# A hand-ordered H3 and spectral mixing kernel: three groups of zero matmuls enter the table, and the whole order is written anew

## The chip, the cores and the metric

The kernel runs on one core of one Trainium2 chip. The metric is the device time of one execution in microseconds (us), the median of several runs. The profile is that of one more execution, with its own time.

The engines are named as in the profile: PE does matmuls (PEld are its weight loads), DVE is the vector engine, ACT the scalar engine, POOL the gpsimd engine, and SP issues most of the DMAs. The clock granted to PE is given as a share of full speed.

## What is computed

The reference mixes two branches by a gate, on a sequence of 2048 tokens with 640 channels, all in float32:

```python
g = sigmoid((x * gate_w).sum(-1))              # x is A_q
k_shift = causal depthwise conv of k, 4 taps
kv = k_shift * v
y = irfft(rfft(kv, 4096) * rfft(ssm_k, 4096))[:2048] + kv * ssm_D
a = q * y                                       # branch A
b = irfft2(rfft2(x) * (w_r + 1j * w_i))         # branch B, over tokens and channels
return g * a + (1 - g) * b
```

## The kernel before

All Fourier transforms are matmuls with constant matrices. A length of 2048 is split into 64 x 32, so each transform has two stages with a 32 x 32 block transpose by DVE between them (L319, L440, L652).

Branch A goes in five chunks c of 128 channels. `kv` (L576) makes the four-tap convolution times v for half a chunk: ACT scales k by each tap (L601) and POOL or DVE adds (L609), or, for chunk 0, ACT starts (L592) and DVE goes on in PSUM (L595); PE transposes the result (L624) and DVE multiplies it with v (L632). `s1` (L638, matmuls L649) is the first stage for kv ("Y") and for the filter ("H"), `amid` (L673, matmuls L685) the second stage and the product of both spectra: ACT copies one part out of PSUM (L694 or L696), and DVE (L700) or POOL (L702) multiplies. `asum` (L705, L709) adds parts, `is1a` (L712, matmuls L314, transpose L319) is the first inverse stage and `afin` (L726, matmuls L744) the second. Its unit "q" loads q and lets ACT scale it by the gate, eight small steps (L733); DVE multiplies with it (L751), and the result is added to the output in DRAM by an accumulating DMA from POOL (L762) or, for the last half of the last chunk, added by POOL to a kept piece (L758) and stored by SP (L760).

Branch B: `dfwd` (L361) is the transform over channels for two of 16 token groups: it loads xT, folds it by symmetric sums and differences (L340; a sum of 512 at L347, differences and sums of 256 at L348, L350 and L351, a small one of 128 through ACT L355 and DVE L356, or DVE alone at L358) and multiplies (16 passes of 128 rows at L371, 16 of 32 rows at L377); ACT copies the result into XX (L387 to L394). Then `b1` (L437, transpose L440), `bs2` (L456, with the weights w), `i1` (L314), and at the end `bfin`: units "u" (L498, L506, copied by ACT L517) and "dic" (L525, L530), whose results `bout` (L540) scales with the gate (ACT L547 to L550, DVE L553), adds (L555, L556, on POOL or DVE) and sends to the output (L568 from SP, L570 from POOL). `gate_cols` (L328 to L334) writes the gate's columns into the constant dfc, so the first fwd needs dfc and these small DVE steps.

The program has 993 steps. Each has a name (a unit such as fwd.4, kv.4.8, amid.3.1.0), one or two engines on which it can run, and buffers: eight PSUM banks ("ps"), eleven "a" buffers of 128 x 1088, five "s", one "k", one for the big constants s2b and is2b ("c1"). `order` (L210) reads the order from TABLE: an entry `i+a/b1/b2<j` issues step i on its alternative a, with its new buffers in slots b1 and b2, and makes it wait for step j. Every engine runs its own steps in that order, each waiting by semaphores for data and buffers; SP's DMA queue is in order too. Nothing is reordered at run time. Some loads that the order moves: xT of a group is 512 KB, dic 403.5 KB, a w 322 KB, a v 512 KB, is2b 2 MB.

At the start, while the first loads are on their way, PE runs 24 matmuls of a zeroed tile `wrm` (two passes each, L773).

Of the kernel before, what the change touches and what calls it, by code (L numbers as in the profile page):

```python
# [31 lines left out]
345/1 152/4/0 41 336/2 39 344 40+1<39 167/3 160/4 123/5 342 31+1/2/1 32 35 159 328/7 34 153 33 155 102+1/0/4 154 42+1/2/6 106/0 157 103+1 16/8 105+1  # L32
158 156 107 104+1 95+1/2/0 324/0 96+1 116/6 49 80+1/1/3 98+1 48 325 99/4 43 81<98 97 46 10/9 100 45 326 44 108/6/4 47 82 83 84/2 85 73+1/2/1 346 77/3
74+1 75<74 78 349/2 327/0 109 115 168/0/4 110 111 347/4 114 350 76 433/1 113 112 348 405/0 169 86+1/0/2 172/6 225/3 9/0 171 173 170+1 161+1/2/0 162+1
165/7 163+1 219/4 329/4/0 8 124+1/1/3 93 245/0 337/2 164<124 166 87 330 290/10 88 4 125 92 90 338 89 126 174/6/4 91 128/0 129 251/5 127 427/7
117+1/2/1 121/1 118+1 119+1 120+1 351/2/1 181 17/0/4 18 122 19+1<18 21 130/4/0 352 20+1 175 176 11/2/0 177 407/2 178 12 180 15 179 13 409/6 136 131
133 134 132 14 22+1/2/6 137 135 353/0 23 29 27 25 28 357/4 24 355/6 26 184/2 358 406/8 356 411/9 408<14 354 192/4 193 416/0 413/2 410 188/6 182 186/0
189 183 412 185 375/4 187 379/6 383/2 376/1 380/6 377 363/0 378 384/3 381+1 190/4 386 364/9 385 365+1 194/2 191 428+1 382+1 429/4/2 195 366+1 417/6
371/6 372/9 430 434+1 246/2 247/2/0 220/0 204/4 374+1 248 221/4/1 373+1 420/0 418/9 437/2 222 7 249 232/4 202/6 438 250 205 414/0/0 419 203 226/2
359/4 415 227/8 224 264/9 360/3 228/0/2 223 422/2 361 229 493/0 362 435/6 200/0 395/1 231 252/2 436 233/4 230 253/3 201 421 387/6 254/1/4 367/0  # L40
234/3/0 235 388/8 368/2 494/0 198/2 258/4 370 390+1 369 431/4 495/7 196/0 389 432 255<389 496 497/8 303/3 284/5 199 197 499/7 498+1 396 393/4 237<498
504/0 424/8 236 423 391/0 500 394 265/4 400/2 285/6 392 501/7 286/2/0 425/0 256 287 397/2 257 426 266/6 267/3/1 288 506/5 289 259/6 515/8 401 398 268
304/0 439/4/1 399 260/4/0 270 297/6 261 445/2 269 440 212/9 305/4 306/2/1 262 443/6 263 441/4 502/0/0 446 442 307 505/1 507 444 298/2 508/3 291/4
206/4 292/0 299/3/0 503 402/6 308 521/5 309 300 510/7 516+1 471/0 293/4/1 301 455/2 403 459/4 302 472/2 294 404 456/0 474 600/0 473 460/6 463/6 458
296 277/0 457 467/0 464/3 461+1 475/2 465 468/10 466 462 213/6 476/2 451/4 469 214/6 470 452/10 477 295<477 215/2/0 447/0 478 207/6 448/3 454+1<478
517/2/0 449 208/1/4 453+1 488/2 450 519/0 209 604/10 216 518 512/4 481/4 601/8 211+1 520 217<211 602/6 522+1 509+1 483/9 606/3 479/0 603+1 210+1 608/6
589/0 482 511<210 489 605 480 278/4 513/6 279/7 591/1 271/10 514 525/0 218 607 590/4 527/2/1 280/3/1 526 523/6 238/5 533/4 528 611/3 281 529/0 484
584/0 534 592 531/2 272/4 593/7 524 490/6 532 595/1 273/4/0 283 282 594 485/2 530 274 491 239/0 597/10 276 486 240/7 241/2/1 551/4 275 487 543/6 492
552/3 596 559/2 553 544/0 554 547/0 560/4 545 242 561 598/4/0 548/1 562 546 617/9 539/2 540/4 550+1 599 696/0 549 555/6 579/5 243+1 704/7 609/4 675/2
# [12 lines left out]
971 939 972 911/6/2 749 950/1 840 940/3 949 750 941 952 973 763+1 909+1/0/0 951 912 764+1 851 942 953 767/4 954 910 980/4<764 943 955/1 944 913+1/0/2
# [117 lines left out]
class _Plan:  # L180
# [41 lines left out]
def _body(ctx, tc, I, out):  # L222
# [21 lines left out]
    def ps(b):  # L244
        return banks[:, b.slot:b.slot + b.banks]
# [3 lines left out]
    mm = nc.tensor.matmul  # L249
# [39 lines left out]
    wrm = cst.tile([128, 128], F32, name="wrm")  # L289
# [286 lines left out]
    def kv(c, h, kvt):  # L576
# [23 lines left out]
        else:  # L600
# [172 lines left out]
            mm(ps(pw)[:, 0, :128], wrm, wrm, start=True, stop=True)  # L773
# [128 lines left out]
```

## Time and profile before

| | |
|---|---|
| median of 3 runs | 289.94 us (288.68 to 290.15) |
| the profiled execution's own time | 291.7 us |
| its span in the profile | 289.9 us |
| mean granted clock of PE | 0.98 |
| busy: PE, DVE, POOL, ACT | 258.9, 225.9, 205.8, 151.4 us |
| moved by DMA | 53.93 MB, mean 186 GB/s |

A row of the timeline reads: start, length, engine, line, operation, output and inputs, shapes, number of instructions, and in brackets how long the engine had been idle and what ended it. A row of the groups by line has the busy time, the mean of one instruction in ns, the idle time before them and its releasers. In the chain of waits, each piece is start, length, and what the end of the kernel hung on at that time.

### The profile page before, as it was taken

The numbers are of one execution on the slowest core, as the hardware profiler recorded it, in microseconds if no ns is written. First come the engines' busy times: TensorE is split into PE (matmuls) and PEld (weight loads), VectorE is DVE, ScalarE is ACT, GpSimd is POOL, SyncE is SP. The second block draws the span as 40 slices with busy tenths as digits, with TensorE's granted clock in tenths as the row PEclk, the third lists the DMA queues.
The fourth block names the chain that finished last, engine by engine and source line by source line (L and its number), as shares of the span: only waits on it lengthen the run. The fifth ranks groups of instructions, "written<-read, shape, count | busy, mean of one in ns | idle before, by whom it ended". The sixth has DMA issues, their size and how long they took to land.

```text
span 289.9 us, 9390 instructions
## 1 busy us (share of the span) xinstructions
PE 258.9 (89%) x4024; PEld 169.9 (59%) x4024; DVE 225.9 (78%) x284; ACT 151.4 (52%) x315; POOL 205.8 (71%) x206
## 2 busy tenths in 40 slices
PE   8784999989999899889999988999998998999750
PEld 8663797534554366534385323678766775888450
DVE  2689698497999799899999999993467857358670
ACT  2238349715456465756655763354594036486710
POOL 1362732367897998776996999858990876889872
PEclk9899799999999999999999999999999999999996
DMA  7999999370155785847558657292003397305788
GB/s 211 418 394 363 379 339 398 109 290 18 49 183 155 249 235 159 287 119 251 175 186 266 257 154 310 79 270 103 3 3 91 93 196 128 54 22 76 111 114 144
DMA packets 25432, 53.93 MB, mean 186 GB/s; under 512 B 1840, under 2 KB 13360, under 8 KB 24880
## 3 DMA queue, kind: packets, MB, share of 16 engines
q1 hardware_dynamic: 22048, 48.63, 48.9%
q0 software_dynamic: 3344, 4.72, 11.7%
q8 instruction: 31, 0.51, 0.7%
q14 instruction: 9, 0.07, 0.1%
HBM read 43.38 MB, written 9.96 MB: 184 GB/s over the span
## 4 chain that ended last, share of the span: by engine, by line
PE 64%; DVE 22%; issue 5%; ACT 3%; DMA 2%; POOL 1%; POOLq 1%; SPq 1%; ACTq 0%; DVEq 0%
PE banks L685 12%; PE banks L649 9%; PE banks L314 7%; PE banks L530 7%; PE banks L498 6%; PE banks L437 5%; PE banks L744 5%; PE banks L371 4%; DVE ZZ L652 3%; DVE XX L319 3%; DVE ZZ L319 3%; DMA a<-xT 2%; PE banks L525 2%; DVE s L468 2%; DVE ZZ L700 2%
## 5 line engine op out<-in xcount | busy, mean ns | idle before, releaser
L609 POOL TENSOR_TENSOR a<-a,a 128x1024 f32<-128x1024 f32 x21 | 50.1, 2392 | 13.7 <-ACT a L601 10.6
L652 DVE STREAM_TRANSPOSE ZZ<-banks 128x1024 f32<-128x1024 f32 x40 | 47.9, 1229 | 9.0 <-ACT XX L391 4.7
L601 ACT ACTIVATE a<-k,one 128x1024 f32<-128x1024 f32 x32 | 35.9, 1149 | 26.2 <-POOL a L609 9.7
L685 PE MATMUL banks<-ZZ,s2a 64*32 64x256 f32 x1280 | 41.0, 387 | 3.5 <-issue 1.3
L702 POOL TENSOR_TENSOR ZZ<-a 128x512 f32<-128x512 f32 x24 | 30.5, 1288 | 12.1 <-ACT a L694 10.9
L685 PEld LDWEIGHTS banks<-ZZ,s2a 64*32 64x32 f32 x1280 | 23.9, 104 | 17.5 <-issue 4.3
L553 DVE SCALAR_TENSOR_TENSOR s<-banks,om,s 128x322 f32<-128x322 f32 x32 | 17.4, 550 | 21.4 <-ACT s L550 20.9
L700 DVE TENSOR_TENSOR ZZ<-banks,s 128x512 f32<-128x512 f32 x40 | 25.3, 682 | 6.1 <-ACT s L696 5.9
L709 POOL TENSOR_TENSOR ZZ<-ZZ 128x512 f32<-128x512 f32 x21 | 26.4, 1283 | 3.0 <-DVE ZZ L700 2.9
L476 POOL TENSOR_TENSOR XX<-s,s 128x320 f32<-128x320 f32 (+1 forms) x29 | 24.3, 858 | 4.3 <-DVE ZZ L700 2.2
L371 PE MATMUL banks<-dfc,s 128*128 128x162 f32 x128 | 22.7, 335 | 4.9 <-POOL s L350 2.9
L314 PE MATMUL banks<-ZZ,one 32*64 32x512 f32 x448 | 26.6, 607 | 0.3 <-DVE XX L319 0.3
L319 DVE STREAM_TRANSPOSE ZZ<-banks 128x2048 f32<-128x2048 f32 x10 | 22.9, 2306 | 4.0 <-PE banks L314 4.0
L694 ACT ACTIVATE a<-banks 128x1024 f32<-128x1024 f32 x20 | 20.4, 1028 | 10.0 <-PE banks L685 9.0
L371 PEld LDWEIGHTS banks<-dfc,s 128*128 128x128 f32 x128 | 20.4, 211 | 7.6 <-POOL s L350 3.1
L733 ACT ACTIVATE a<-a,g 128x128 f32<-128x128 f32 x80 | 24.3, 391 | 0.9 <-DMA a<-q 0.9
L649 PE MATMUL banks<-a,one 64*128 64x512 f32 x80 | 21.1, 615 | 3.1 <-DVE ZZ L319 1.6
L744 PE MATMUL banks<-ZZ,is2a 128*64 128x128 f32 x320 | 19.5, 277 | 3.1 <-ACT a L733 2.8
L744 PEld LDWEIGHTS banks<-ZZ,is2a 128*64 128x64 f32 x320 | 18.1, 134 | 5.8 <-ACT a L733 3.7
L649 PE MATMUL banks<-kvt,one 64*128 64x512 f32 x80 | 20.0, 616 | 0.2 <-ACT a L694 0.2
L437 PE MATMUL banks<-XX,two 64*128 64x464 f32 (+1 forms) x88 | 19.8, 582 | 0.1
L530 PE MATMUL banks<-dic,s 128*128 128x161 f32 x128 | 19.6, 305 | 0.0
(83 smaller groups left out, 474.9 us busy)
## 6 DMA issues: line engine op xcount, KB each, us to landing
a<-xT SPq DMA_DIRECT2D x16, 512.0 KB, 9.6
k<-k SPq DMA_DIRECT2D x10, 704.0 KB, 5.3
a<-h SPq DMA_DIRECT2D x10, 544.0 KB, 5.1
a<-w SPq DMA_DIRECT2D x16, 322.0 KB, 3.8
a<-v SPq DMA_DIRECT2D x10, 512.0 KB, 5.8
a<-q SPq DMA_DIRECT2D x10, 512.0 KB, 4.9
out_dram<-a SPq DMA_DIRECT2D x8, 512.0 KB, 4.7
out_dram<-a POOLq DMA_DIRECT2D x16, 256.0 KB, 5.9
```

Source lines behind the costliest of these rows:

```text
L314: mm(p[h * 64:h * 64 + 64, j, :nd * 8], is1[r, c, :], v[r, h * 2 + ri, :, d0:d0 + nd, :].rearrange("p m d e -> p d m e"), start=(i == 0), ...
L319: nc.vector.transpose(by_col(x, d0, nd), p[:, :, :nd * 8].rearrange("p j (d i) -> p d j i", i=8))
L371: mm(v(q)[:, i, :CB], sb(f, 5, 128)[:, x], dfc[:, x], start=first and i == 0, stop=True, skip_group_check=True)
L437: mm(v()[:, b], m1b[r, ri], xv[r, ri, d0:d0 + nd], start=ri == 0, stop=ri == 1)
L530: mm(v(q)[:, i, :161], sb(u, 5, 128)[:, q], dic[:, q * 161:q * 161 + 161], start=first and i == 0, stop=True, skip_group_check=True)
L601: tap = lambda t, j: op([("ACT", act_us(1024), lambda: act(sb(t, 8, 128), K(j), AF.Copy, scale=sh[:, c, j:j + 1]))], r=[k, "one"], w=[t], ...
L609: either(1024, lambda o: o(sb(ts[x], 1024), sb(ts[x], 1024), sb(ts[y], 1024), op=OP.add), r=[ts[y]], w=[ts[x]])
L649: mm(ps(p)[:, b], m1[r], v[r], start=True, stop=True)
L652: op([("DVE", dve(1024), lambda: nc.vector.transpose(by_col(Z(z), u * 32, 32), ps(p).rearrange("p b (d n) -> p d b n", n=16)))], r=[p], w= ...
L685: apart(c, m, "mid", mm(ps(p)[j * 32:j * 32 + 32, h].rearrange("p (y r d) -> p y r d", y=2, r=2)[:, :, ri], s2a[r, k, ri * 32:ri * 32 + 32 ...
L700: alts = [("DVE", dve(512), lambda x=x, dst=dst, hv=hv: tt(dst(), V(part(ps(p), zy)), hv(), op=OP.mult))]
L744: mm(v[b * 64:b * 64 + 64, j, :], is2a[:, n2, :], row(Z(zh), n2), start=True, stop=True)
```

## The change

Three units "fill" are added behind the warm-up. Each runs five matmuls of the zeroed tile (ten passes) into a PSUM bank that nothing else reads. As they are declared right after steps 0 and 1, every later step has its number raised by three: step 64 becomes 67.

```diff
+FILL = 3
...
     pe(8.6, warm, "F", r=["wrm"], w=[pw], new=[pw])
+    for i in range(FILL):
+        unit("fill", i)
+        pf = new("ps")
+
+        def fill(pf=pf):
+            for _ in range(5):
+                mm(ps(pf)[:, 0, :128], wrm, wrm, start=True, stop=True)
+
+        pe(1.15, fill, "F", r=["wrm"], w=[pf], new=[pf])
```

The table is new from the first entry to the last. Its beginning and end:

```diff
-57/0 0 1/0 3 5 2 50/1 145/2 331/0 138/3 339/4 36/5 94/6 58+1/0/1 30/7 101/8 59+1 62/1 61+1 79/9 63 60<61 6 51+1/2/3 55/2 52+1 53+1 56 54+1 146+1/4/0
-64/4/6 150/3 147<146 151 148 149 139/2/4 332/0 333 334 71 143/2 65 66 67 140 340+1 70 144 69 335/10 341/6/0 68 142 141 37/1/3 38 323/0 343/2 72/0
...
+60/0 6 53/1 5 8 148/2 0 1/0 4/1 61+1/0/1 65/2 66 62<61 64+1 334/0 141/3 63<64 342/4 39/5 33/6 97/7 104/8 54+1/2/3 55+1 57+1 56<57 58/3 59 9 82/9
+149+1/4/0 150+1 152<150 151 153/4 154 142/2/4 143 67/6/2 335/0 336 337 146/5 147 73 343+1 344/4/0 144+1 145+1 74 346/2 40/1/3 68 69 70 72 41+1<40 43+1
...
+106+1 107+1 108+1 110 160 159 98+1/2/0 99+1 339/6 83+1/1/3 100+1 248/8 327/0 102/6 103 328 329 2/7 101<100 52 111+1/2/6 119/7 46 48 50 47 49 84 86 85
...
-880 945/6 981 768 946 956 957 948 914 769/4 915/1 947 916 917 958 918 925/0 924 919 926 983 927 770 985 920/9 982 922 921 928 923 929 930+1/8 881/0
-931+1 933 986/4 882 932<931 883 988 987 991+1 989+1 992 990
+923/7 924 772/4 773 931 932 926 933+1/8 934+1 936 3/2 935+1 925+1 950<925 884/2 885 886 960 989/4 990 992+1 993 991 994+1 995
```

Steps 2, 3 and 4 of the new numbering are the fills: 4 stands right behind the warm-up (bank 1), 2 between the matmuls of fwd.2 and fwd.8 (bank 7), 3 between is1.4.1 and afin.4.0 (bank 2). Read by unit, the rest changes as follows.

- PE keeps its sequence of stages; neighbours trade places (b1.1 before b1.0, amid.0.0.1 before amid.0.2.1, afin.3.8 before afin.3.0, and many more such pairs).
- The first five loads were fwd.5's xT, two, dfc, one, fwd.4's xT, and are now fwd.5's xT, two, fwd.4's xT, one, dfc. The loads of dic, of w for bs2.0.6 and of v for kv.0.8 now stand ahead of the xT of fwd.10, fwd.1 and fwd.0.
- 30 steps change between DVE and POOL. Thirteen of them are folds of the first fwd; the others are products and sums of amid, asum, bs2, kv.2.0 and dic. At the end, two small steps of dic.10 and dic.11 (L556) go from POOL to DVE, ahead of afin.4.0's product (L751), and one of dic.13 (L556, POOL) comes between afin.4.0's store and the last two additions (L758).
- The loads of q.4.0 and q.4.8 and their ACT scalings move forward. q.4.8 is scaled among the taps of kv.4.8, ahead of two of them, and q.4.0 after those of kv.4.0, ahead of amid.3.1.0; before, q.4.0 was scaled ahead of ACT's steps of dic.10 and q.4.8 as ACT's last step. On SP, is2b, q.4.0 and q.4.8 now stand ahead of q.2.8, q.2.0, h.3.1, h.3.0 and the k of kv.4.0.

No arithmetic on the data changes.

More of the change, by code (lines that the diff above doesn't have):

```diff
@@ L34 @@
[L34 to L49, printed above, removed]
@@ new lines @@
+173+1 164+1/2/0 168/7 165+1 169 166+1 167+1 96 95 13/1 7 228/0 254/3 127+1/1/3 128<127 129 130 90 92 93 94 91 332/0/0 333 340/6 341 430/2 416/5
+177/2/0 222/10 12/0 131/4 132 120+1/2/1 124/5 121+1 123+1 122+1 183 184 20/0/4 21 23+1<21 22+1 24 354/6/1 125 133/0/4 178 182 181 179 180 355 410/4
+409/6 14/2/0 15 18 17 16 25+1/2/6 134 135 137 138 136 411<16 140 356/4 357 139 32 360/0 26 31 27 358/6 359 29 10 28 361 30 189/4 195/2 191/6 185 190
+192 196 366/0 412/7 413 414/9 415 419/0 382/4 367/1 368 383/4 369+1<368 378/6 379/2 381 187/2 188 193/0 186 385+1 436/7 197/2 421/9 431+1 380 432/6/2
@@ new lines @@
+420/1 422 423/9 194 374/0 384+1 375/4 198 223/2 249/4 433 424 425/9 496/0 377+1 224/1/3 225 227 306/10 250/0/4 251 235/8 376+1 253 207/6 208 205/2 206
+226 252 434/4 435 417/6/0 418 229/0 427/2 370/2 255/4 230/4 231/2/1 232 234 233 371/3 373 372 256/6 257/0/4 258 386/6 387/3 388 389 203/0 204 267/5
+236/2 237/3/1 238 497/0 398/4 362/4 363/2 364 365 390/6 199/0 437+1 440/2 438/4 391/3 426 200 201/0 439 500/6 502/8 392+1 498/9 287/7 393+1 394/4
+261/3 499 501 240 503 441 260 507/0 508/9 239 518/6 519+1 202 396/0 399 395 268/4 288/6 397 259 403/8 289/2/1 290 291 292 504/7 428/0 429 269/1
@@ new lines @@
+270/3/0 271 509/2 510 273 300/1 272 400/2 401 402 293/5 262/6 263/4/1 264 266 265 404 442/0/1 443 446/4 444/2 445 448/6 449 511/3 307/0 308/2 309/2/0
+310 505/2/0 506 215/4 311 301/6 302/3/1 294/0 295/0 405/2 447 466/4 513/7 603/0 491/2 303 474/6 312 296/4/0 462/0 305 304 406 407 297 299 467/2 469
+468 475/1 477 476 463/10 209/1 458/2 459/3 460 461 464+1 465 470/4 471/0 473 472 478/6 479/5 481 298<481 216/2 217/10 218/2/1 480 454/0 455/8
+457+1<480 456+1 605/0 210/4 211/3/0 212 214 450/2 451/4 453 452 524/5 520/6/0 521 522/4 523 484/0 482/4 219 492 280/1 486/8 274/6 525+1 515/4 512+1
@@ new lines @@
+701/0 988 575 705/10 631 582/8 628/4 629 323/0 324 620/7 313/4 314 321/0 322 583 319/4 320 573 574 700/4 571 317/0 318 572 621+1 588 570 614/6 615+1
+315/4 316 688/0 702 690/0 704 689/2 706 691 692/10 694/0 883 580/0 581 578/4 579 616/0/1 622/2 623 624/4 618/6 625 617 589/2 584/4 619 642/0 643/1
+634/6 635/3 693 695 707/7 590 646/2 591 647/6 585 654/4 645 644 658/0 716/10 637 636 697/6/0 586 649 648 669<648 668 857/2/2 659/0 660 661 855+1/0/4
+655/0 657+1 656+1 858 698 678/3 856 708/6 709 638/2 639/6 640+1 641+1 666 667 650/0 651/1 653 652 670 671 859/6/4 861/3 860 803/0/0 801+1/2/1 872/2
@@ new lines @@
+862 710/2 863 804 722/0/0 864 865 871 874 873 662/6 875 876 877/8 879 878 880 723 802 805/2/4 663/5 665+1 664 673<664 806 683/4 818/4 776/0/2 817
+774+1/6/0 807/1 819 820 821 777 724/0 808 809 728/2 822 810 811 725 729 775 684 672 676/4 677 866/7 679 674/0 778+1/4/6 780/0 790 791/2 793 779 782
+781 812/0 814 813 815 867 711+1 675 685/0 686 687 680/2 712/0/2 868 783 717+1 792 726/4 794 681 720/2 682 795 796/6 798 784 889/6/1 727 887+1/4/3
+785/5 786 787 789 797 800 799 823/4 825 788 713 718/0 888 824 714/4 890 870 721 891/2/6 893/0 892 902 816 827 719 830/0/2 715 894 964+1/4/4 895 896
@@ new lines @@
+897 900/3 898/10 899 831 903/1 904 905 906 907 910 908/2 826 965 909 754/0 755/3 757 756 881 730/2 731/0 732 733 742/4 743/5 744 745 734/6 735/6
+737+1<745 901 738/0 739/3 741 740 736 763+1 911 758/2 759/0 760 761 769<761 828/4/1 829 962+1/0/0 963 764 832+1/6/4 844 845/3 765 966/2/0 834/1 762
+846 847 848 849 850/4 833 835 836 837 838 937/6/2 967 968/0 977 970 969 851+1 852<851 853 938 939+1/4/4 839/5 746/6 869 978/3 979 980 750/2 768 940
+841 840 842 971 972 973/6 975 981 982 747/1 748 749 974 751/8 752+1 753+1 766+1 767+1 976 843 983/0<767 941+1/4/0 952 942 953/0 943/1 955 954 944 945
```

22 lines of the change are left out of this document (7 added, 15 removed).

## The prediction

> **What bounds the kernel now.** I read the page first: the shares of the engines and the chain that ended last.
>
> ```profile
> span 289.9 us, 9390 instructions
> PE 258.9 (89%) x4024; PEld 169.9 (59%) x4024; DVE 225.9 (78%) x284; ACT 151.4 (52%) x315; POOL 205.8 (71%) x206
> PE 64%; DVE 22%; issue 5%; ACT 3%; DMA 2%; POOL 1%; POOLq 1%; SPq 1%; ACTq 0%; DVEq 0%
> ```
>
> PE is the first limit (64% of the chain), DVE the second (22%). PE stands still for 289.9 - 258.9 = 31 us, and the page's line of the granted clock dips twice in the first 36 us. Next I read the timeline of PE there, then the table of short windows around each drop (columns: length, busy time of PE, its weight loads, DVE, ACT, POOL, then granted clock, DMA share, GB/s).
>
> ```profile
> 1.06 7.68 PE L773 MATMUL banks<-wrm 128*128 128x128 f32 x48 [1.06 <-DVE wrm L768]
> 10.75 3.81 PE L371 MATMUL banks<-dfc,s 128*128 128x162 f32 x16 [2.01 <-DVE s L350]
> 14.49 1.38 PE L377 MATMUL banks<-dfc,s 32*128 32x164 f32 x16
> 18.67 2.47 PE L371 MATMUL banks<-dfc,s 128*128 128x162 f32 x16
> 22.88 0.84 PE L377 MATMUL banks<-dfc,s 32*128 32x164 f32 x16 [0.97 <-DVE s L358]
> 29.00 4.14 PE L371 MATMUL banks<-dfc,s 128*128 128x162 f32 x16 [2.88 <-POOL s L350]
> ```
>
> ```profile
> 12.00:12.50 0.50, 0.50 (x5) 0.50 (x4) 0.16 (x1) 0.45 (x2) 0.50 (x1) 0.73 0.99 407
> 15.50:16.00 0.50, 0.37 (x8) 0.05 (x4) 0.50 (x1) 0.06 (x1) 0.50 (x1) 0.86 1.00 401
> 29.00:29.50 0.50, 0.50 (x3) 0.50 (x4) 0.50 (x1) 0.14 (x1) 0.50 (x1) 0.79 0.97 393
> 32.50:33.00 0.50, 0.50 (x4) 0.40 (x2) 0.50 (x1) 0.00 (x0) 0.50 (x1) 0.79 1.02 418
> 285.00:286.00 1.00, 0.00 (x0) 0.00 (x0) 0.00 (x0) 0.00 (x0) 0.00 (x0) 0.65 1.41 203
> ```
>
> A unit fwd (16 wide passes of L371, 16 narrow ones of L377) takes 2.47 + 0.84 = 3.3 us at full clock. After the rest of 2.01 us the wide part took 3.81 and the narrow one 1.38; after the rest of 2.88 us the wide part took 4.14. At half clock a window reads 0.73 when 0.54 of it is slow, so the clock fell at 12.23 and came back at 15.64, then fell at 29.29 and came back at 32.71: both spells last 3.4 us. They cost 1.34 + 0.54 = 1.9 us and 1.67 us of PE. The last row puts a third fall at 285.30, when PE is done. What ended these rests is DVE and POOL preparing inputs, so I read DVE's pace off the chain of waits in order of time (start, us, what) and the groups by line for the steps that change engine.
>
> ```profile
> 17.15 1.27 DVE a L595
> 20.02 1.02 issue
> 21.05 1.21 DVE ZZ L652
> 23.50 0.60 DVE s L347
> 24.10 0.34 DVE s L348
> 24.81 0.28 DVE s L356
> 27.57 0.65 issue
> 49.11 0.84 PE banks L377 x16
> 55.17 3.34 PE banks L437 x16
> ```
>
> ```profile
> L351 POOL TENSOR_TENSOR s<-s 128x256 f32<-128x256 f32 x9 | 6.6, 734 | 7.0 <-DVE s L347 4.5 <-DVE s L350 2.4
> L347 POOL TENSOR_TENSOR s<-a 128x512 f32<-128x512 f32 x3 | 3.8, 1272 | 0.0
> L556 POOL TENSOR_TENSOR a<-s 128x128 f32<-128x128 f32 (+1 forms) x31 | 17.3, 611 | 3.0 <-ACT s L517 2.6 <-DVE s L553 0.4
> L556 DVE TENSOR_TENSOR a<-s 128x190 f32<-128x190 f32 x1 | 0.3, 350 | 0.0
> ```
>
> The 512 fold advances DVE by 0.60, a 256 fold by 0.34, the small fold by 0.28, the taps of L595 by 1.27, a transpose of L652 by 1.21. On POOL a 256 fold costs 0.73 and a 512 fold 1.27.
>
> **The change, opening.** Nearly every step is the same instruction in another place; 30 steps change between DVE and POOL, and the DVE folds before the last fwd come to about the same sum (seven 256 folds go to POOL; five, and one 512 fold, come back). So I follow the chain of fwd.4, fwd.12, fwd.2, fwd.8 in the new order.
>
> ```profile
> 8.20 0.16 DVE L330 TENSOR_TENSOR dfc<-gs 128x2 f32<-128x2 f32 x1
> 8.60 0.32 DVE L334 TENSOR_TENSOR dfc<-gs,two 64x1 f32<-64x1 f32 x2
> 9.21 0.69 DVE L347 TENSOR_TENSOR s<-a 128x512 f32<-128x512 f32 x1 [0.29 <-DMA a<-xT]
> 12.29 1.12 ACT L592 ACTIVATE banks<-k,one 128x1024 f32<-128x1024 f32 x1
> ```
>
> Before, the fifth load, fwd.4's xT, is in at 9.21 and its folds follow. In the new order the same five loads end with dfc, fwd.4's folds are done by then, and only the gate columns follow, which ran from L330 at 8.20 to the end of the L334 pair at 8.92: 0.7 us, so fwd.4 starts at 10.0 instead of 10.75. The first fill is ten passes like the 48 of 7.68 us: 1.6 us at that mean. The warm group ends at 8.74, so the rest of 2.01 us all but goes and the clock should hold: fwd.4 ends at 13.3, not 15.87. fwd.12 needs the second bank pair of kv.0.8, freed by the L595 step that ends at 18.42 before. New order: the first fold of fwd.13, and ACT's copies behind it, come some 1.1 earlier, so that L592 ends at 12.3 instead of 13.41; then on DVE 2 x 1.27 + 0.28 + 2 x 0.34 + 0.60 + 1.27 = 5.4, so 17.7 against 18.67 (-1.0). fwd.2: 0.28 + 1.21 + 0.60 + 0.34 + 1.21 = 3.6 later, 21.3 against 22.88 (-1.6), ending at 24.6. The second fill follows at once; its bank 7 is read last by ACT's copies of fwd.12, which I place before 24. fwd.8: the folds of fwd.9, fwd.8 and the first of fwd.7 on DVE, 3 x 0.60 + 6 x 0.34 + 0.28 = 4.1, so 25.4, and POOL's last fold 0.73: 26.1 against 29.00 (-2.9). At full clock it ends at 29.4, where before 29.00 + 4.14 + 0.84 less the overlap is 33.9 (-4.5).
>
> From there DVE is almost without a pause. Adding its steps in the new order up to fwd.0's last fold gives 45.5, where before the last fold ends after 49.11, and PE, then in one piece, reaches the first b1 near 51.4 against 55.17. **The gain of the opening** lies between nothing and 3.8. My sum has none of the short hand-over gaps that the chain calls issue (two of them, 1.02 and 0.65, stand above), so I hold 1.0 back: -2.8. Of the DMAs, dic, a w and a v now stand ahead of fwd.10, fwd.1 and fwd.0: 403.5 + 322 + 512 KB at the 407 GB/s of the first window row, 3 us later for those xT. What hides it is that their folds are the opening's last ones; without that cover up to 3 us would return.
>
> [...]
>
> **The change, middle.** Between 55 and 266 the order differs by neighbours trading places.
>
> ```profile
> 137.00:182.00 45.00, 41.65 (x710) 20.66 (x708) 44.51 (x40) 25.51 (x44) 42.37 (x31) 1.00 0.65 223
> 161.69 1.15 ACT L601 ACTIVATE a<-k,one 128x1024 f32<-128x1024 f32 x1 [0.85 <-DMA k<-k]
> 163.72 2.46 ACT L733 ACTIVATE a<-a,g 128x128 f32<-128x128 f32 x8 [0.89 <-DMA a<-q]
> 174.57 4.85 POOL L609 TENSOR_TENSOR a<-a,a 128x1024 f32<-128x1024 f32 x2
> 189.16 0.60 ACT L696 ACTIVATE s<-banks 128x512 f32<-128x512 f32 x1 [4.61 <-PE banks L685]
> ```
>
> The one large move is q.4.0 and q.4.8: two loads and 16 ACT scalings (2.46 us a group) go from the end to this stage. The loads stand on SP behind is2b and ahead of q.2.x, h.3.x and kv.4.0's k. On ACT, q.4.8 now stands ahead of two taps of kv.4.8; the last tap would end at 161.69 + 4 x 1.15 + 2 x 2.46 = 171.2, and POOL asks for it only at 174.57. q.4.0 falls into ACT's rest of 4.61 before 189.16. I cost it at nothing, with 3.4 us of cover; bounds 0 and +4.9. For the other exchanges of the middle I take 0, and keep +-1.0 for the range, one hand-over like the issue of 1.02 above gained or lost.
>
> **The change, end.** The timeline of the last stage:
>
> ```profile
> 266.58 2.08 PE L314 MATMUL banks<-ZZ,one 32*64 32x512 f32 x32
> 274.19 2.31 DVE L319 STREAM_TRANSPOSE ZZ<-banks 128x2048 f32<-128x2048 f32 x1
> 276.64 3.85 PE L744 MATMUL banks<-ZZ,is2a 128*64 128x128 f32 x64 [2.81 <-ACT a L733]
> 278.71 1.22 DVE L751 TENSOR_TENSOR a<-banks,a 128x1024 f32<-128x1024 f32 x1 [0.40 <-PE banks L744]
> ```
>
> The row of L744 names ACT's scaling, which the new order has done long before; but DVE's transpose of is1.4.1 ends at 274.19 + 2.31 = 276.50, as late, so the scaling that goes frees 0.1 at most, and DVE is late next. The third fill stands in PE's rest of 2.81 and waits only for bank 2, which ACT has read before it begins its scaling: nothing. The clock did not fall after this rest (the 64 passes took 3.85; it fell only at 285.30). DVE gets two small L556 steps of at most 0.35 ahead of L751; 0.40 of rest takes all but 0.3, and since the sizes are smaller than the row's I count 0.1. POOL gets one L556 step between the last accumulating store and the two last additions: 0.61 by the group's mean, and the last two stores wait for these additions: +0.6. Bounds 0 and +1.0. Together +0.7.
>
> **Sum.** -2.8 + 0 + 0.7 = -2.1 against the profiled execution's own time of 291.7 (its span of 289.9 and 1.8 around it), so 289.6 in those terms; that execution lay 1.76 over the median of 289.94, so for the median 289.94 - 2.1 = **287.8 us**.
>
> **Rivals.** *The clock near the end (-).* The falls at 12.23, 29.29 and 285.30 lie 17.06 and 256.01 apart, 5 and 75 times 3.41: they sit on one grid. On it an edge lies at 285.30 - 3 x 3.41 = 275.06, inside the rest of 2.81, and cuts it into parts of 1.2 and 1.6. Where the grid lies otherwise, the whole rest falls between two edges and the end of before is slow as fwd.8 was, by 1.67; the third fill takes that away. With the opening's full 3.8: 289.94 - 3.8 + 0.7 - 1.67 = 285.2. [...]
>
> *POOL starved by the moved scaling (+).* Place: ACT at 161 to 175, where DVE (44.51 of 45) and POOL (42.37 of 45) are full. ACT is in order; if q.4.8's load lands late, because it has to get a buffer of the eleven "a" and stands behind 2 MB of is2b, the taps of kv.4.8 wait behind it. From the point where the last tap ends after 174.57, that is over 3.4 us late, POOL waits for each further microsecond, with asum.3 and is1.3 behind it. Price: two groups of 2.46 on the path, 4.9, since both engines are full: 287.8 + 4.9 = 292.7. For it: the row of 163.72 waited 0.89 for such a load already. Against it: the cover.
>
> *The opening brings nothing (0).* If DVE, the xT that land later, or hand-overs take back what the clock gives, -2.8 falls away: 289.94 + 0.7 = 290.6. For it: DVE gets no less work. Against it: DVE's own waits there are for PE and ACT. [...]
>
> **How the numbers follow.** Forecast 0.42, between 286.0 and 289.4 (of it 0.35 faster, 0.07 the same; 0.5% is 1.45 us, about what a measurement of this kernel can tell from no change). Clock near the end 0.13, all faster. POOL starved 0.30, all slower. Opening without gain 0.15, of it 0.11 the same and 0.04 slower. So faster 0.48, same 0.18, slower 0.34. Cases of both signs hold most of the chance; the range goes from 284.9, just under the first rival, to 292.9, over the second.
>
> **What would show it.** Right: fwd.4 near 10.0 and fwd.8 near 26, both with wide parts of 2.5 us, no fall of the clock before 40 us, first b1 near 52, and an end that keeps the shift. Wrong: wide parts of 4 us in spite of the fills; b1 still at 55; a wait of POOL's L609 for ACT between 170 and 190, or of PE's L314 near 215; DVE's last L319 much later against is1.4.1 than 0.4 us.

## The result, and the profile after

| | before | after |
|---|---|---|
| median of 20 runs each, same chip | 290.07 us (288.68 to 291.40) | 290.09 us (288.44 to 292.03) |
| after / before, 95% interval | | 1.0001 (0.9980 to 1.0022) |
| profiled execution: span | 289.9 us | 289.7 us |
| mean granted clock of PE | 0.98 | 0.99 |

A gain of 2.1 us was forecast, and there is none. The page of the changed kernel (span; busy time; granted clock of PE in 40 slices; the instruction queue; the chain by engine):

```profile
span 289.7 us, 9447 instructions
PE 261.0 (90%) x4054; PEld 171.5 (59%) x4054; DVE 226.6 (78%) x286; ACT 151.2 (52%) x315; POOL 206.7 (71%) x204
PEclk9999999999999999999999999999999999999996
q8 instruction: 32, 0.52, 0.7%
PE 31%; DVE 6%; issue 1%; POOL 1%; ACT 0%; POOLq 0%; DVEq 0%
```

In this profile the clock holds through the opening. The chain is followed back to 179 us only, so its shares add up to some 40%; the timelines have to be laid side by side instead. PE's timeline after, at the places that matter:

```profile
8.00 1.28 PE L783 MATMUL banks<-wrm 128*128 128x128 f32 x10
10.29 2.44 PE L372 MATMUL banks<-dfc,s 128*128 128x162 f32 x16 [1.02 <-POOL s L351]
...
26.52 1.38 PE L783 MATMUL banks<-wrm 128*128 128x128 f32 x10
27.83 0.84 PE L378 MATMUL banks<-dfc,s 32*128 32x164 f32 x16
28.60 2.47 PE L372 MATMUL banks<-dfc,s 128*128 128x162 f32 x16
...
52.39 3.93 PE L438 MATMUL banks<-XX,two 64*128 64x464 f32 x18
...
118.72 0.84 PE L686 MATMUL banks<-ZZ,s2a 64*32 64x256 f32 x17 [1.46 <-issue]
...
197.55 0.54 PE L526 MATMUL banks<-dic,s 32*128 32x163 f32 x3 [0.32 <-issue]
...
244.24 2.01 PE L686 MATMUL banks<-ZZ,s2a 64*32 64x256 f32 x53 [1.84 <-issue]
...
273.69 1.38 PE L783 MATMUL banks<-wrm 128*128 128x128 f32 x10 [0.67 <-ACT s L551]
275.96 3.85 PE L745 MATMUL banks<-ZZ,is2a 128*64 128x128 f32 x64 [0.88 <-DVE ZZ L320]
```

The two rows of before that answer to these and were not shown yet:

```profile
55.01 1.41 PE L437 MATMUL banks<-XX,two 64*128 64x464 f32 x6
...
246.08 1.29 PE L685 MATMUL banks<-ZZ,s2a 64*32 64x256 f32 x33 [1.31 <-issue]
```

(Lines of the changed kernel are one higher: L685 is L686 there, L744 is L745.) The first b1 comes at 52.39 instead of 55.01: **the opening gained 2.62 us**, and the lead is still there at 195.8 us, where kv.4.8's last step on DVE ends 2.86 us earlier than before. Then it goes. From b1 to the last L745 the changed kernel takes 275.96 - 52.39 = 223.57 us, before 276.64 - 55.01 = 221.63: **1.94 given back in the middle**. From the start of the last L745 to the end it is 13.74 against 13.28: **0.46 in the tail**. The sum, -2.62 + 1.94 + 0.46, is the -0.2 between the spans.

What holds PE in the middle carries the name "issue": it waited for nothing that the profile shows. The groups by line between the first b1 and the last L745, after and before (busy, mean ns, idle time before them and what ended it):

```profile
L686 PE MATMUL banks<-ZZ,s2a 64*32 64x256 f32 x1280 | 43.2, 388 | 4.6 <-issue 3.6 <-DVE s L469 0.5 <-DVE XX L441 0.4
```

```profile
L685 PE MATMUL banks<-ZZ,s2a 64*32 64x256 f32 x1280 | 41.0, 387 | 3.5 <-issue 1.3 <-DVE XX L440 1.2 <-ACT s L696 0.8
```

3.6 us of "issue" ahead of L686 where before had 1.3, at the same 1280 matmuls. The question for the experiments was what that is.

### The profile page after: what moved, and what is told of

The parts are those of the page before. It is cut to its first block, busy times and chain, and to the rows that moved or that the text cites. A ratio compares the mean times of both kernels' runs of the same rounds, so it can differ in the third digit from the quotient of the medians.

```text
span 289.7 us, 9447 instructions
## 1 busy us (share of the span) xinstructions
PE 261.0 (90%) x4054; PEld 171.5 (59%) x4054; DVE 226.6 (78%) x286; ACT 151.2 (52%) x315; POOL 206.7 (71%) x204
## 5 line engine op out<-in xcount | busy, mean ns | idle before, releaser
L610 POOL TENSOR_TENSOR a<-a,a 128x1024 f32<-128x1024 f32 x22 | 52.4, 2386 | 11.2 <-ACT a L602 5.4
L686 PE MATMUL banks<-ZZ,s2a 64*32 64x256 f32 x1280 | 43.2, 388 | 4.6 <-issue 3.6
L703 POOL TENSOR_TENSOR ZZ<-a 128x512 f32<-128x512 f32 x23 | 29.3, 1290 | 9.6 <-DVE ZZ L701 7.9
L686 PEld LDWEIGHTS banks<-ZZ,s2a 64*32 64x32 f32 x1280 | 23.7, 104 | 20.2 <-issue 8.3
L650 PE MATMUL banks<-a,one 64*128 64x512 f32 x80 | 21.0, 616 | 3.4 <-POOL a L661 2.2
L372 PE MATMUL banks<-dfc,s 128*128 128x162 f32 x128 | 19.9, 306 | 2.8 <-DVE s L351 1.6
L556 POOL TENSOR_TENSOR a<-s 128x322 f32<-128x322 f32 x15 | 12.1, 809 | 14.2 <-DVE s L554 12.9
L697 ACT ACTIVATE s<-banks 128x512 f32<-128x512 f32 x20 | 12.0, 599 | 18.2 <-PE banks L686 13.9
L745 PE MATMUL banks<-ZZ,is2a 128*64 128x128 f32 x320 | 19.8, 277 | 1.2 <-DVE ZZ L320 0.9
L372 PEld LDWEIGHTS banks<-dfc,s 128*128 128x128 f32 x128 | 17.8, 189 | 5.0 <-DVE s L351 2.0
L745 PEld LDWEIGHTS banks<-ZZ,is2a 128*64 128x64 f32 x320 | 18.0, 134 | 4.4 <-DVE ZZ L653 2.4
```

The lines of the kernel that those rows point to most:

```text
L372: mm(v(q)[:, i, :CB], sb(f, 5, 128)[:, x], dfc[:, x], start=first and i == 0, stop=True, skip_group_check=True)
L610: either(1024, lambda o: o(sb(ts[x], 1024), sb(ts[x], 1024), sb(ts[y], 1024), op=OP.add), r=[ts[y]], w=[ts[x]])
L650: mm(ps(p)[:, b], m1[r], v[r], start=True, stop=True)
L686: apart(c, m, "mid", mm(ps(p)[j * 32:j * 32 + 32, h].rearrange("p (y r d) -> p y r d", y=2, r=2)[:, :, ri], s2a[r, k, ri * 32:ri * 32 + 32 ...
L703: alts.append(("POOL", pool_us(512), lambda x=x, dst=dst, hv=hv: ptt(dst(), V(part(sb(hs, 2, 512), zy)), hv(), op=OP.mult)))
L745: mm(v[b * 64:b * 64 + 64, j, :], is2a[:, n2, :], row(Z(zh), n2), start=True, stop=True)
```

## What the waits called issue have in common

I counted PE's records (matmuls, weight loads, its sequencer's own) from the start of the trace to each wait. The three above stand at counts 3009, 5825 and 7106, that of before at 7105: all are 193 or 194 beyond a multiple of 256. The page lists 32 packets on the queue "instruction", 0.52 MB, so 16 KB each, for some 8,170 records: one packet for 256 of them. A packet's place in time can be read from the DMA view of a short window, here 241.8 to 242.0 us of the changed kernel:

```profile
q0 software_dynamic: 9, 0.02, 45.2%
q8 instruction: 1, 0.02, 30.6%
```

In the trace that packet begins at 241.87. The chain of waits has the wait from 242.40 to 244.24:

```profile
238.12 4.27 PE banks L686 x118
242.40 1.84 issue
244.24 2.01 PE banks L686 x46
```

So PE goes on 2.38 us after the packet began. That gave theory C, a reading of these counts alone: PE's instructions come in blocks of 256 records, one packet of 16 KB each, the next block is fetched while one runs, and PE stands still when the fetch begins too late. In this execution the waits at such counts, those three and one of 0.30 at 1730, sum to 3.9 us.

The rivals: A, the opening's gain is real and lost later; B, the opening's slow spells were an accident of one profile; D, the waits are dependencies of the new order; then, for the whole, E (the change is worth its 2 us, hidden by where the code lies) and F (it is worth nothing anywhere).

## Experiments

The runs were made at different times and on different chips; each is judged by its ratio to before, which ran beside it on the same chip.

| run | median us | ratio to before (95%) |
|---|---|---|
| before_again | 290.8 (one) | |
| after_no_fills | 290.36 | 0.9979 (0.9951 to 1.0007) |
| after_warm_8x384 | 287.59 | 0.9887 (0.9846 to 0.9927) |
| after_warm_48x64 | 301.51 | 1.0366 (1.0318 to 1.0414) |
| before_warm_8x384 | 290.25 | 1.0025 (0.9999 to 1.0052) |
| after_no_last_fill | 291.02 | 1.0046 (1.0023 to 1.0069) |
| after_8x384_tail | 287.34 | 0.9928 (0.9899 to 0.9957) |
| after_warm_16x192 | 290.70 | 1.0047 (1.0019 to 1.0075) |
| before_last_fill | 289.39 | 0.9981 (0.9956 to 1.0006) |
| before_warm_16x192 | 289.95 | 1.0008 (0.9986 to 1.0030) |
| before_warm_12x256 | 289.51 | 1.0010 (0.9983 to 1.0036) |
| after_warm_12x256 | 288.94 | 0.9969 (0.9940 to 0.9997) |
| after_q18_later | 290.86 | 1.0016 (0.9983 to 1.0049) |
| best_8x384_tail_q18 | 286.00 | 0.9864 (0.9822 to 0.9905) |

And what their profiles show, each from one execution: the start of the first b1, the way from there to the last L745 (L744 before), that group's length, the span, and the sum of the waits called issue over 0.25 us that end at a count of 193 or 194 modulo 256.

| profile | first b1 | b1 to L745 | L745 | span | issue |
|---|---|---|---|---|---|
| before | 55.01 | 221.63 | 3.85 | 289.9 | 1.31 |
| before_again | 54.48 | 220.56 | 3.85 | 289.0 | 0.54 |
| before_last_fill | 54.63 | 219.61 | 3.85 | 287.5 | 0.54 |
| before_warm_16x192 | 53.83 | 220.00 | 5.33 | 287.9 | 0 |
| before_warm_12x256 | 54.42 | 220.78 | 5.33 | 289.6 | 0.36 |
| before_warm_8x384 | 54.52 | 220.14 | 5.46 | 288.2 | 0 |
| after | 52.39 | 223.57 | 3.85 | 289.7 | 3.92 |
| after_no_fills | 52.31 | 223.03 | 5.42 | 289.5 | 3.42 |
| after_no_last_fill | 52.69 | 222.45 | 3.85 | 287.8 | 2.56 |
| after_warm_16x192 | 52.43 | 225.21 | 3.85 | 291.0 | 5.02 |
| after_warm_12x256 | 52.34 | 222.47 | 3.85 | 288.1 | 2.11 |
| after_warm_8x384 | 52.31 | 220.08 | 3.85 | 286.4 | 1.53 |
| after_8x384_tail | 52.04 | 220.91 | 3.85 | 285.9 | 2.52 |
| after_warm_48x64 | 64.35 | 220.91 | 3.85 | 299.7 | 2.48 |
| after_q18_later | 52.02 | 224.94 | 3.85 | 290.2 | 3.86 |
| best_8x384_tail_q18 | 52.31 | 219.30 | 3.88 | 284.5 | 0.40 |

### Was the profile of before an accident?

before_again, no edit.

> The kernel before, unchanged, profiled a second time. Theory A (the gain of the opening is real and is given back after 197 us): the profile again shows the wide parts of fwd.4 and fwd.8 at 3.8 and 4.1 us and the first b1 at 55.0 within 0.5, and again a wait that the chain calls issue of about 1.3 us at the matmul with number 7105 of PE's stream (matmuls and weight loads counted together). Theory B (the two slow spells of the opening were an accident of one execution, so most executions had nothing to gain): at least one of the two units runs at 2.5 us and the first b1 comes over 1 us earlier.

Both slow spells stood again: fwd.4's wide part 4.21 us, fwd.8's 4.07, the first b1 at 54.48. The wait at count 7105 stood again too, but at 0.54 instead of 1.31 us. So the opening did have something to gain (A), B falls for this order, and the size of an issue wait differs between executions of the same code.

### The fills alone, and the place of the code

after_no_fills:

```diff
-            for _ in range(5):
+            for _ in range(0):
                 mm(ps(pf)[:, 0, :128], wrm, wrm, start=True, stop=True)
```

> The new order with the three groups of zero matmuls empty (60 PE instructions fewer; the order, the slots and all else as in the changed kernel). Theory A: without fills the clock drops again in the rests ahead of fwd.4 and of fwd.8, wide parts of 3.8 to 4.1 us, the first b1 between 53.5 and 55 instead of 52.4, and the time 0.5 to 1.5 us over the changed kernel unless other waits move. Theory B (the order alone brings the opening its gain): b1 stays at 52.4 and the time is the same. The theory that the waits called issue sit at fixed distances in PE's instruction stream (theory C) expects that they leave amid.4 at 244 us and sit 60 instructions further on in the work, at the same count of 7105; a dependency of the new order (theory D) expects the 1.84 us at the same matmul of amid.4.

PE's timeline of this run:

```profile
10.54 2.44 PE L372 MATMUL banks<-dfc,s 128*128 128x162 f32 x16 [1.68 <-DVE dfc L332]
...
15.89 3.74 PE L650 MATMUL banks<-a,one 64*128 64x512 f32 x8 [2.14 <-POOL a L661]
...
275.33 5.42 PE L745 MATMUL banks<-ZZ,is2a 128*64 128x128 f32 x64 [3.02 <-DVE ZZ L320]
```

Without fills fwd.4 still runs at full clock after a rest of 1.68 us. One slow spell falls on an L650 (3.74 where the changed kernel took 2.35), and the first b1 still comes at 52.31. So in this profile the order makes the opening's gain, not the two fills there. The other profiles agree. With both of these fills the clock still fell at 15.8 to 17.3 us in three of them (after_warm_12x256, after_no_last_fill, after_q18_later), in a rest of some 2.2 us ahead of an L650 where no fill stands, and b1 came at 52.02 to 52.69 all the same. Near fwd.8 the clock fell in all six profiles of the order before, at 27.8 to 30.1 us, and in none of the changed order, with the fills or without them. The third fill matters: without it L745 took 5.42 instead of 3.85 here. And C's first test came out: the waits again ended at counts 1730, 3010, 5569 and 7106, though 40 instructions were gone ahead of them.

after_warm_8x384 and after_warm_48x64 move the code without touching its work, by cutting the warm-up otherwise:

```diff
-        for _ in range(WARM):
-            mm(ps(pw)[:, 0, :128], wrm, wrm, start=True, stop=True)
+        for _ in range(8):
+            mm(ps(pw)[:, 0, :384], wrm[:, :128], wrm, start=True, stop=True)
```

(wrm gets 384 columns for it, which also shifts the tiles that are laid out behind it; that was not tried by itself. The other kernel runs 48 matmuls of `wrm[:, :64]`, with wrm as it was.)

> The changed kernel with its warm group cut otherwise: 8 matmuls of 384 columns in place of 24 of 128, the same columns in all but 64 PE instructions fewer ahead of everything else; no other difference. Theory C (PE stands still at fixed counts of its instruction stream, 193 or 194 beyond a multiple of 256): the waits called issue leave amid.4 at 244 us and dic.6 at 197 us and are found, if at all, at other units, again at counts 193 or 194 modulo 256; the time moves by up to 2 us either way. Theory D (waits of the new order): the waits of 1.84 and 0.32 us stay at the same matmuls of amid.4 and dic.6, now at counts 64 lower, and the time stays within 0.5 us.

> The changed kernel with 48 warm matmuls of 64 columns in place of 24 of 128: 96 PE instructions more ahead of everything else, the same columns. Theory C: the waits called issue sit at other units but at the same counts modulo 256, and the time moves by up to 2 us either way. Theory D: they stay at amid.4 and dic.6, at counts 96 higher, and the time stays within 0.5 us.

64 instructions fewer took 1.1% off: 287.59 us, with not a single instruction of the work changed. The wait in amid.4 shrank from 1.84 to 0.26, in place of the 1.46 in amid.1 there is one of 0.48 ahead of an L457 one count on (3010), that of dic.6 went, and one of 0.79 came up in an L507:

```profile
191.07 0.30 PE L507 MATMUL banks<-c,XX 128*32 128x64 f32 x3 [0.79 <-issue]
...
272.39 3.85 PE L745 MATMUL banks<-ZZ,is2a 128*64 128x128 f32 x64 [0.88 <-DVE ZZ L320]
```

Its count is 5569 = 21 x 256 + 193. D falls. The 48 matmuls of 64 columns were a mishap as a test of position: the warm-up took 20.74 us instead of 7.10, and the first b1 came at 64.35. PE's timeline shows what was slow:

```profile
1.06 20.74 PE L774 MATMUL banks<-wrm 128*128 128x64 f32 x96 [1.06 <-DVE wrm L769]
21.60 2.45 PE L783 MATMUL banks<-wrm 128*128 128x128 f32 x10
```

The ten passes of the first fill, which have 128 columns, took 2.45 us behind it where the changed kernel took 1.28. The first record of a granted clock, a full one, begins at 24.91 us in this trace and at 4.2 to 7.3 us in the other fifteen. So the clock was not up during this warm-up; why it stayed down is open. But the run shows that a delay of the opening is carried: +11.96 at b1, -2.66 from there to L745, +10.0 in the span.

### The same edits on before; the third fill; the tail

before_warm_8x384 has the edit above on the kernel before.

> The kernel before with the warm group of 8 matmuls of 384 columns: its whole PE stream 64 instructions earlier, nothing else. The same edit took the changed kernel from 290.1 to 287.6 us, and the waits called issue from 3.9 us in all to 1.5. Theory E (the change is worth its 2 us, hidden by where the code lies): before stays at 290 within 0.8, or falls by less than the changed kernel did, so that at this position the changed kernel is ahead by 1.5 to 2.5 us. Theory F (the edit helps both kernels alike and the change is worth nothing at any position): before falls to 287.6 within 0.7 as well.

290.25 us: the edit that gave the changed kernel 1.1% gave before nothing. F falls: at this position the changed kernel is ahead by 2.7 us in the medians and 1.4% in the ratios, more even than the 1.5 to 2.5 us of E. Its profile has no issue wait at all, though; what it won there it lost at the end, where the clock fell:

```profile
274.66 5.46 PE L744 MATMUL banks<-ZZ,is2a 128*64 128x128 f32 x64 [2.81 <-ACT a L733]
```

The rest of 2.81 us is the same one after which the first profile of before had 3.85: the clock fell behind it in one execution and not in the other.

after_no_last_fill empties the third group alone:

```diff
-            for _ in range(5):
+            for _ in range(0 if i == 1 else 5):
```

> The changed kernel with its third group of zero matmuls, the one ahead of the last L745, left empty; every instruction before it keeps its place. If that group holds the clock up, L745's 64 passes take 5.4 us instead of 3.85 in the profile, as they did when all three were empty, and the time is up to 1.6 us longer; where the clock falls only in some executions, the median is 0.3 to 1.6 us longer. If the rest ahead of L745 does not let the clock fall, 3.85 us and the same time.

+0.45 points in the ratio, 1.3 us. The profiled execution kept 3.85, so the clock falls there in some executions only. Over all profiles without this group, it fell in four of seven (5.33, 5.33, 5.46, 5.42); with the group, in none of nine. before_last_fill gives the group to the kernel before, ahead of its last L744:

> The kernel before with one thing of the change alone: the group of ten zero passes ahead of the last L744; nothing before it moves. Without that group the changed kernel was 1.3 us slower. If the clock falls in the rest ahead of L744 in most executions of the kernel before too, it gets 0.8 to 1.5 us faster; if its rest of 2.81 us (against 3.00) mostly leaves the clock up, as the two profiles of before show, less than 0.4 us.

0.9981: 0.55 us, at the edge of what can be told. By the two, and by 4/7 x 1.54 = 0.9 from the profiles, the third fill is worth 0.5 to 1.3 us.

after_8x384_tail moves one entry of the table, dic.13's addition on POOL (960), from behind the last accumulating store to ahead of dic.11's:

```diff
-926 933+1/8 934+1 936 3/2 935+1 925+1 950<925 884/2 885 886 960 989/4 ...
+926 933+1/8 934+1 960 936 3/2 935+1 925+1 950<925 884/2 885 886 989/4 ...
```

> The changed kernel with the 8 warm matmuls of 384 columns, and with dic.13's addition (L557) on POOL moved from between the last accumulating store and the two last additions to ahead of dic.11's store. If that step delayed the two last additions, the second of them ends 4.1 us after the start of the last accumulating store (L763) instead of 4.4, and the time is 0.3 to 0.6 us under the 287.6 us of the same kernel without the move; if the additions wait for DVE's L752 anyway, no change.

POOL's timeline at the end, in the changed kernel and in this one:

```profile
279.57 1.57 POOL L763 DMA_DIRECT2D out_dram<-a  x1 [0.24 <-DVE a L752]
280.54 1.04 POOL L557 TENSOR_TENSOR a<-s 128x128 f32<-128x128 f32 x1
280.92 3.09 POOL L759 TENSOR_TENSOR a<-a,a 128x512 f32<-128x512 f32 x2
```

```profile
276.56 1.57 POOL L763 DMA_DIRECT2D out_dram<-a  x1 [0.24 <-DVE a L752]
277.54 3.10 POOL L759 TENSOR_TENSOR a<-a,a 128x512 f32<-128x512 f32 x2
```

From the store's start to the end of the additions it takes 4.44 us in the changed kernel and 4.08 in this one: 0.36 us. The kernel before has 4.08 as well (280.24 to 284.32). The times cannot confirm it: the median, 287.34, is 0.25 under that of after_warm_8x384, but the ratio, 0.9928, is over its 0.9887, and the two intervals overlap. So the step rests on these rows alone.

### More positions

16 matmuls of 192 columns (32 instructions fewer) and 12 of 256 (48 fewer), for both kernels:

> The changed kernel with 16 warm matmuls of 192 columns: 32 PE instructions fewer ahead of everything else, the same columns. Theory C (PE stands still at fixed counts of its stream, 2.2 to 2.5 us after the start of a 16 KB packet on the instruction queue): the waits called issue again end 2.2 to 2.5 us after such a packet, at other matmuls than in the changed kernel by 32 records; the sum of these waits tells the time: 290.1 less 3.9 plus that sum, within 0.8 us. Theory D (waits of the new order): 1.46 and 1.84 us at the same matmuls of amid.1 and amid.4 as in the changed kernel, and 290.1 us.

> The kernel before with 16 warm matmuls of 192 columns, 32 PE instructions fewer ahead of everything else. At the three positions so far before stood at 290.1 and 290.3 (0 and 64 fewer) and the changed kernel at 290.1, 290.7 and 287.6 (0, 32 and 64 fewer). If the change is worth about 2 us and the place of the code adds a lottery of 0 to 4 us, before stands here between 289 and 292, and the waits called issue in its profile again end 2.2 to 2.5 us after an instruction packet; if place moves only the changed kernel, 290 within 0.3.

> The kernel before with 12 warm matmuls of 256 columns, 48 PE instructions fewer. A lottery of code position: between 289 and 292; the mean of the four positions is what the changed kernel's mean is to be held against.

> The changed kernel with 12 warm matmuls of 256 columns, 48 PE instructions fewer. Theory C: between 287 and 291, by 290.1 less 3.9 plus the sum of its waits called issue, within 1 us; over four positions the changed kernel's mean is 0.5 to 2 us under that of before. If the change is worth nothing, the two means agree within 0.3 us.

The changed kernel's ratios at 0, 32, 48 and 64 fewer: 1.0001, 1.0047, 0.9969, 0.9887, with issue sums of 3.92, 5.02, 2.11, 1.53: the time goes with the sum. Before: 1, 1.0008, 1.0010, 1.0025, with sums of 1.31, 0, 0.36, 0. The means are 0.9976 and 1.0011, so over positions the change is worth about 0.35%, 1.0 us (each ratio is known to 0.2 to 0.4%); where the code happens to lie is worth up to 1.6% to the changed kernel and almost nothing to before, which stayed at 290 within 0.6 at all four, with the same widths of wrm. The expectation by the sum (290.1 - 3.9 + sum) gave 291.2 and 288.3 for the two; the ratios make 291.4 and 289.2.

### Why the packets come late

In all fifteen profiles but after_warm_48x64 I took each packet's start less the moment when PE's count passed 193 + 256 k, with the busy share of the DMA engines in the 2 us around that moment: 439 packets. Where the share was under 25%, the median was 0.1 us; from 95% on, 2.3 us (nine in ten under 3.8). This shows that the two go together, not yet that one makes the other. In amid.1 that moment was followed by the packet after 0.6 to 1.4 us in before's six profiles, and after 2.7 to 4.1 us in seven of the changed order. Its DMAs at that place on SP, and what the windows show (length, busy PE, its loads, DVE, ACT, POOL, clock, DMA share, GB/s):

```profile
111.18 0.33 SPq L581 DMA_DIRECT2D k<-k  x1
111.61 0.60 SPq L730 DMA_DIRECT2D a<-q  x1
114.07 0.40 SPq L765 DMA_DIRECT2D out_dram<-a  x1
114.56 0.53 SPq L448 DMA_DIRECT2D a<-w  x1
```

```profile
112.00:114.00 2.00, 2.00 (x88) 1.35 (x75) 2.00 (x4) 0.60 (x1) 1.70 (x3) 1.00 0.88 214
114.00:116.00 2.00, 2.00 (x80) 1.31 (x72) 2.00 (x5) 1.90 (x3) 1.92 (x3) 1.00 1.01 399
116.00:118.00 2.00, 1.21 (x39) 0.24 (x19) 2.00 (x4) 1.25 (x2) 1.70 (x2) 1.00 1.11 355
```

The load of q at 111.61 is q.1.8's, which before issued at 125.23. Theory I: it stands in the packet's way. Both runs put it behind the w of bs2.0.0:

```diff
-... 603/0 491/2 303 ... 209/1 458/2 ...
+... 603/0 303 ... 209/1 491/2 458/2 ...
```

> The changed kernel with one load moved on SP: q.1.8's 512 KB from behind the k of kv.3.8 (issued at 111.6 us) to behind the w of bs2.0.0 (114.6 us). Theory I (instruction packets wait behind bulk transfers): the packet that began at 116.3 us begins at 115.3 or before, the wait of 1.46 us in amid.1 at 119 falls under 0.4 us, and the median is 0.5 to 1.5 us under the changed kernel's 290.1. Rival (the packets come late anyway, the order before only hid it behind other waits of PE): the packet at 116 and the wait at 119 stay within 0.4 us of what they were, the time too.

> The fastest version so far (8 warm matmuls of 384 columns, dic.13's addition moved on POOL, 287.3 us) with q.1.8's load moved in the same way. Its profile had a wait of 2.12 us in amid.1 at 119. Theory I: that wait falls under 0.4 us and the time to between 285.5 and 287.0 us, the fastest of all. Rival: 287.3 us within 0.5.

SP and PE in after_q18_later:

```profile
114.52 1.77 SPq L448 DMA_DIRECT2D a<-w  x1
116.38 0.40 SPq L730 DMA_DIRECT2D a<-q  x1
```

```profile
117.78 0.82 PE L457 MATMUL banks<-XX,c 64*32 64x161 f32 x32
118.36 1.14 PE L686 MATMUL banks<-ZZ,s2a 64*32 64x256 f32 x32
...
123.44 1.06 PE L686 MATMUL banks<-ZZ,s2a 64*32 64x256 f32 x18 [1.95 <-issue]
```

The packet began at 114.73 instead of 116.33 and the wait at 119 went, as expected. The time did not follow: the next packet, now beside the load that had been moved, began at 121.20, 4.2 us after PE had come to its block, and the same wait stood one block later, 1.95 us at count 3265. Behind that wait the clock fell as well: the window from 126 to 127 us reads 0.50, and the L650 at 124.42 took 3.21 us where the changed kernel took 1.99. after_no_last_fill has such a fall too, behind its wait of 1.77 us at 118.95 (0.50 from 120 to 123); no figure for issue counts this loss. In the other kernel that next block found its packet in time (118.47); its one wait left is 0.40 us, and it is the **fastest of all, 286.0 us, 0.9864 (0.9822 to 0.9905)** of before:

```profile
span 284.5 us, 9381 instructions
PEclk9999999999999999999999999999999999999997
```

The rival (late packets that before only hid) falls for amid.1: the same packet came 1.6 us sooner when one load moved, and 2.8 us sooner in the other kernel (113.89, where after_8x384_tail has 116.72). In amid.4 no load was moved. From PE's coming to that block until its packet began, the queue of POOL's accumulating stores (software_dynamic) took 94.5% of the DMA engines' time in the changed kernel (238.13 to 241.87) and 76.9% in before (240.70 to 243.65). That they delay the packet there is by analogy, not tried.

Over the sixteen profiles 33 issue waits ended at counts of 193 or 194 modulo 256 and 2.18 to 2.49 us after an instruction packet began. None of PE's other issue waits over 0.25 us after the first such packet, at 17 to 25 us, was left over.

## Why the prediction was wrong

The step that failed is the one on the middle: "For the other exchanges of the middle I take 0, and keep +-1.0 for the range". It cost 1.94 us in the compared pair and 2.1 on average (b1 to L745: 222.53 over seven profiles of the changed order, without those of after_warm_48x64 and of the moved load, 220.45 over the six of before), with issue waits of 3.0 against 0.5 us. I had read the wait of 1.31 us in before as a thing of its own and asked of each moved load only who waits for its data, not what it stands in front of.

- **Opening, -2.8:** right in size. b1 came at 52.39 (foretold near 52), 2.62 earlier in the pair, 2.1 on average (54.48 to 52.36). fwd.4 was at 10.29 (10.0), but fwd.2 at 23.35 (21.3) and fwd.8 at 27.83 (26.1). Two terms of my sums were wrong there: ACT's L593, whose last wait was for the load of k, ended at 13.23 instead of 12.3, and ahead of fwd.2 DVE ran two small folds at L359 of 0.70 and 0.85 us, where the sum has a single one of 0.28. The reason was wrong in part: what the fills were to save at the clock is not what brought b1 forward, as it came at 52.31 without them and at 52.02 to 52.69 where the clock fell in spite of them. The order makes the gain; that the two fills of the opening add to it is not shown.
- **q.4's moved scalings, 0:** right; the lead was 2.86 at 195.8 us, past everything that could have waited. The rival "POOL starved" did not happen.
- **End, +0.7:** 0.46 in the pair; POOL's step is 0.36 of it instead of 0.61.
- **The clock near the end:** the fall is real, 4 of 7 profiles without the third fill, 1.5 us each. The grid of 3.41 us holds too: in before_warm_8x384 the falls at 29.71 and 275.47 lie 245.76 us apart, 72 times 3.413, and in the changed kernel the first record of a clock at 4.18 and the fall at 284.07 lie 279.89 apart, 82 times 3.413. That the place of the rest on this grid decides whether the clock falls was my estimate; it was not tried by itself. In the profile that I read, the end lay well, and I gave it 0.13. Averaged, it is 0.5 to 1.3 us, which I had at nothing.
- **"The opening brings nothing":** 290.6 was the nearest of my cases to 290.09, for another reason.

So on average: -2.1 (opening), -0.9 (third fill), +2.1 (middle, where the issue waits alone are +2.5), +0.4 (POOL's step). That makes -0.5 against 0.0 measured at this position and -1.0 as the mean of four. It also stays open why the rest of the middle, without these waits, is some 0.5 us shorter, and what part the turned order of dic.12, u.10 and u.11 has (8.15 us instead of 7.80 in the pair between 257 and 266); that was not tried.

## What to carry to other kernels

When a wait on PE is called issue, count PE's instructions up to it: where several stand at one remainder of 256, as the 33 here at 193 or 194, look at the packets of the instruction queue; these waits ended 2.18 to 2.49 us after one began. In amid.1 one load in the way delayed it by 1.6 and 2.8 us in two kernels, so a load's place can have a price even if nobody waits for its data. Judge a reordering of a kernel like this at several positions of the code: a warm-up cut into fewer, wider matmuls moves it without touching the work and here was worth 1.1% (8 of 384 columns) against 0.35% for the whole change, as long as the warm-up keeps its length (7.27 us there, 7.10 uncut). And where the clock falls behind a rest in some executions only, as behind the 2.81 us ahead of L744 in three of five profiles of before, one profile can show either case.

## What the runs showed of the hardware

- Identical work took 287.6 us with 64 PE instructions fewer ahead of it and 290.7 us with 32 fewer; the waits called issue in the two profiles sum to 1.53 and 5.02 us, each of 0.26 to 1.48.
- Behind issue waits of 1.77 and 1.95 us the clock read 0.50 in two profiles (after_no_last_fill, 120 to 123 us; after_q18_later, 126 to 127).
- Behind the same rest of 2.81 us the same 64 passes took 3.85 us in two profiles of before and 5.33 to 5.46 in three.
- In after_warm_48x64 a warm-up of passes of 64 columns did not bring the clock up: 96 passes took 20.74 us (216 ns each) and ten of 128 columns right behind them 2.45 us, with a full clock on record only from 24.91 us. In the changed kernel 48 passes of 128 columns took 7.10 us (148 ns each), with a full clock from 4.18 us. What makes the difference was not tried.
